# A written-out order for the last four attention units and the last two routing chunks

## The chip, the cores and the metric

The kernel runs on one core of one Trainium2 chip. The metric is the device time of one execution in microseconds (us); the time before is 531.47 us, the median of three runs (531.43 to 533.45).

## The reference

Three steps follow one another, all in fp32. First attention with 4 batches, 8 heads, 768 positions and head width 64: each query sees the 96 keys up to itself and the first 8 keys, with a linear bias in the distance. Its output, 3072 tokens of width 512, goes through a soft mixture of 8 experts with 4 slots each. Its result goes through a feed-forward network with hidden width 2048 and a squared ReLU.

```python
logits = x @ phi                              # 3072 x 32
d = np.exp(logits - logits.max(0)); d /= d.sum(0) + 1e-09
slot_input = d.T @ x                          # 32 x 512
for e in range(E):                            # 8 experts, 4 slots each
    h = np.maximum(slot_input[e] @ w1[e], 0.0)
    slot_out[e] = h @ w2[e]
c = np.exp(logits - logits.max(1)); c /= c.sum(1) + 1e-09
x = c @ slot_out
g = np.maximum(x @ w_in, 0.0) ** 2
out = g @ w_out
```

The softmax `d` runs over all 3072 tokens, so no slot input is final before the last token's attention is done.

## The kernel before

The schedule is manual: each engine works through its instructions in the order in which the program writes them, and waits are put in between for data and for the reuse of tiles.

Attention is cut into 48 units: a batch, a pair of 128-row query tiles, and a pair of heads. Four units (all heads) make a chunk of 256 tokens, so there are 12 chunks; chunk 10 holds units 40 to 43, chunk 11 units 44 to 47. A unit goes through these stages: `stage_qk` (TensorE: scores, line 223), `stage_max` (VectorE: mask and minimum, L236), `stage_exp` (ScalarE: exponentials and their sums, L251), `stage_T` (TensorE: transposes of the probabilities sm, L262), `stage_ev` (VectorE and ScalarE: copies of them out of PSUM, L268), `stage_pv` (TensorE: products with the values, L279), and `stage_x` (ScalarE: copy into the chunk's xT, L289). The loop at L544 takes two units at a time and runs the scores some four units ahead.

`route(k)` (L312) takes a finished chunk to the slots. It is a generator: `queue` and `step(n)` (L489 to 497) place its parts between those of the units. Its steps:

- the logits: products of xT and phi (pt or lt, L351, for an ordinary chunk, copied by L354 and L355 and transposed into pl, L361; directly into pl, L325, for the last chunk);
- the reciprocals rc of the softmax sums (L365, L366), the scaling of the logits by them (L384, or L337) and the head sum into c_tok (L340);
- the turn of xT back to token rows (px, L330) and its scaling into xb (L333);
- pq (L402 or L405), the transposed logits; their running maximum (L420, L421), the exponentials dT and the factor fo for what was summed before (L424, L425);
- pd (L437 or L439), dT transposed back, copied into db (L447); the denominators rden (L456);
- pS (L464), the slot products of db and xb, added to acc with the factor fo (L484).

Odd chunks only do the first three and keep their xb, in the pool `att`; even chunks do the rest for two chunks at once. For chunk 10 (`LAST`) the maximum of its slots is also brought to one row and back (pn, row, pm: L434, L459, L467). Chunk 11 is the tail: `route(11, True)` computes its logits in two halves behind all value products, and then, in the block "last" (L629), pq, dT, pd, the slot products in two matmuls of 512 columns, the sum of acc and pS (L476), and pv (L478), which turns the slot inputs and divides by the denominators. One copy (L479) places them in slotZ, from which the expert products (L654) read. `warm` (L76) issues idle bf16 matmuls; the tail has three, four and six of them (L410, L444, L471).

PSUM has eight banks here: four with tag "s" (scores, and the tail's extra tiles, `bank(..., True)`) and four with tag "m" (all else). Tiles of one tag take its banks in turn, and a new tile waits for the last reader of the one that it replaces.

In SBUF, the pool `att` holds sm (three of 4 KB a partition), raw (queries and keys, four of 3 KB), the value tiles va and vb (two each of 2 KB), pTa and pTb (4 KB each) and the odd chunk's xb; its tags are placed in the order in which they are first asked for: sm, raw, va, pTa, ... Once it is released (L619), the pool `stream` takes its room: s0, s1, s2, each 16 KB a partition, for the second to fourth w2 weights, and slotZ. With `reuse_waits="tile"` each of these waits for the tiles that it lies over. The weight loads (`load_w`, L193; 2 MB each) stand one behind the other on the sync queue (SP): three after the attention, then one behind each expert's products, the last one (w2 of expert 7) in four parts.

## Time and profile before

| what | value |
|---|---|
| median of three runs | 531.47 us |
| the profiled execution | 532.31 us |
| its span, first to last instruction | 530.5 us |
| its mean granted TensorE clock | 0.999 |
| TensorE matmuls busy | 515.5 us, 97% |
| VectorE busy | 383.4 us, 72% |
| ScalarE busy | 306.3 us, 58% |
| GpSimd busy | 167.8 us, 32% |

All times in the views are us from the start of the span, unless marked ns. PE is TensorE, PEld its weight loads, DVE VectorE, ACT ScalarE, POOL GpSimd, SP the sync engine's DMA queue. A row of the timeline merges like instructions that follow one another (x16), with the time from the first's start to the last's end. In brackets stands the idle time of the engine ahead of it and what ended it. An fp32 product shows as two records, a transpose as one. The attention runs to about 177 us, the rest of the routing to 188.9, the experts to about 223, and the feed-forward network from 229 to the end.

### The profile page before, as it was taken

The page shows a single profiled execution, that of the slowest core. Times are in us where ns is not written, and L with a number is a line of the kernel's source. Part 1 is how long each engine was busy: PE and PEld are TensorE (multiplying, and loading weights), DVE is VectorE, ACT ScalarE, POOL GpSimd, SP SyncE. Part 2 cuts the span into 40 slices and gives each one's busy share as a digit, 9 for nine tenths or more (in the row PEclk, how much of TensorE's full clock was granted, in tenths as well). Part 3 has the DMA queues.
Part 4 walks back from the last instruction along what each step waited for, and adds up shares of the span by engine and source line. Part 5 has one row for each costly group of instructions (what it writes and reads, how often), then busy time and mean ns, then how long its engine had stood idle before and what let it go on. Part 6 is the DMA issues. An engine that isn't in the chain of part 4 may idle for free.

```text
span 530.5 us, 10062 instructions
## 1 busy us (share of the span) xinstructions
PE 515.5 (97%) x3628; PEld 392.4 (74%) x3628; DVE 383.4 (72%) x936; ACT 306.3 (58%) x814; POOL 167.8 (32%) x146
## 2 busy tenths in 40 slices
PE   8999999999998899999999999999999999999997
PEld 5787777677776634377787888878888878888885
DVE  5788888787877844778969897967947667545553
ACT  4987877878787201376665655545635445444440
POOL 7000000000000010034674576446554537534441
PEclk9999999999999999999999999999999999999999
DMA  8879999999991799904123021030110000003333
GB/s 281 265 265 314 355 326 342 312 362 314 334 337 43 280 388 416 396 32 160 38 122 121 38 75 84 1 120 0 48 72 1 0 1 1 1 1 120 119 120 119
DMA packets 25977, 89.18 MB, mean 168 GB/s; under 512 B 2882, under 2 KB 3522, under 8 KB 23874
## 3 DMA queue, kind: packets, MB, share of 16 engines
q1 hardware_dynamic: 25776, 88.35, 45.8%
q8 instruction: 30, 0.49, 0.4%
q14 instruction: 25, 0.20, 0.1%
q10 hardware_dynamic: 146, 0.13, 0.1%
HBM read 82.18 MB, written 6.29 MB: 167 GB/s over the span
## 4 chain that ended last, share of the span: by engine, by line
PE 50%; DVE 9%; ACT 1%; issue 1%; POOL 1%; DVEq 0%; POOLq 0%
PE acc L866 14%; PE acc L867 14%; PE acc L868 14%; PE h L848 3%; DVE cvyi L758 1%; DVE rg L853 1%; PE pSO L747 1%; DVE cvyi L757 1%; DVE cvyo L758 1%; DVE oacc L872 1%; PE pre L654 1%; DVE cvyo L757 1%; PE pu L807 1%; DVE winf L761 1%; DVE oacc L874 1%
## 5 line engine op out<-in xcount | busy, mean ns | idle before, releaser
L856 POOL TENSOR_TENSOR g<-rg,g 128x512 fp32r<-128x512 f32 (+1 forms) x109 | 135.1, 1242 | 164.6 <-DVE rg L853 159.6
L866 PE MATMUL acc<-w,g 128*128 128x512 f32 x384 | 151.7, 395 | 1.0 <-DVE oacc L872 1.0
L868 PE MATMUL acc<-w,g 128*128 128x512 f32 x384 | 150.1, 391 | 0.7 <-POOL g L856 0.7
L867 PE MATMUL acc<-w,g 128*128 128x512 f32 x384 | 150.7, 392 | 0.0
L852 ACT ACTIVATE rg<-h 128x512 f32<-128x512 f32 (+1 forms) x109 | 59.7, 548 | 122.2 <-PE h L848 116.0
L874 DVE TENSOR_TENSOR oacc<-acc,oacc 128x512 f32<-128x512 f32 x95 | 65.3, 687 | 58.7 <-PE acc L868 58.7
L251 ACT ACTIVATE sm<-sm,nm 128x256 f32<-128x256 f32 (+1 forms) x192 | 92.8, 488 | 0.3 <-DVE nm L236 0.3
L868 PEld LDWEIGHTS acc<-w,g 128*128 128x128 f32 x384 | 72.1, 188 | 18.5 <-POOL g L856 2.8
L866 PEld LDWEIGHTS acc<-w,g 128*128 128x128 f32 x384 | 72.1, 188 | 17.7 <-DVE oacc L872 1.8
L867 PEld LDWEIGHTS acc<-w,g 128*128 128x128 f32 x384 | 72.4, 189 | 11.1
L853 DVE SCALAR_TENSOR_TENSOR rg<-h,rg 128x512 f32<-128x512 f32 (+1 forms) x109 | 67.8, 622 | 17.2 <-ACT rg L852 17.1
L236 DVE CUSTOM_DVE_ANT_0 sm<-s,mask 128x256 f32<-128x256 f32 (+1 forms) x192 | 66.9, 395 | 3.3 <-ACT sm L251 1.7
L855 ACT ACTIVATE g<-rg 128x512 fp32r<-128x512 f32 (+1 forms) x109 | 63.4, 582 | 3.5
L223 PE MATMUL s<-raw 64*128 64x256 f32 (+1 forms) x384 | 52.6, 394 | 0.7 <-DMA raw<-in_qk 0.7
L628 POOL MEMSET slotZ<- 128x1056 f32 x1 | 1.0, 978 | 155.3 <-DVE nm L236 155.3
L262 PE MATMUL pt<-con,sm 128*128 128x128 f32 x352 | 45.2, 276 | 1.6 <-ACT pT L268 1.6
L279 PE MATMUL o<-pT,v 128*64 128x128 f32 x704 | 44.2, 276 | 0.8 <-issue 0.5
L279 PEld LDWEIGHTS o<-pT,v 128*64 128x64 f32 x704 | 37.9, 137 | 7.9 <-DVE nm L236 2.2
L262 PEld LDWEIGHTS pt<-con,sm 128*128 128x128 f32 x352 | 38.5, 141 | 6.8 <-ACT pT L268 2.8
L223 PEld LDWEIGHTS s<-raw 64*128 64x128 f32 x384 | 31.2, 191 | 15.5 <-DMA v<-in_vx 6.7
L848 PEld LDWEIGHTS h<-cu 128*128 128x128 f32 x192 | 35.8, 188 | 7.4
L848 PE MATMUL h<-cu 128*128 128x256 f32 x192 | 39.8, 280 | 0.0
(166 smaller groups left out, 546.0 us busy)
## 6 DMA issues: line engine op xcount, KB each, us to landing
w<-in_w SPq DMA_DIRECT2D x40, 512.0 KB, 6.7
raw<-in_qk SPq DMA_DIRECT2D x48, 384.0 KB, 5.7
v<-in_vx SPq DMA_DIRECT2D x48, 256.0 KB, 4.5
w<-in_w SPq DMA_DIRECT2D x6, 2048.0 KB, 13.0
out_x<-oacc SPq DMA_DIRECT2D x23, 256.0 KB, 2.0
win<-in_w_in SPq DMA_DIRECT2D x2, 2048.0 KB, 8.9
wout<-in_w_out SPq DMA_DIRECT2D x2, 2048.0 KB, 7.8
win<-in_w_in SPq DMA_DIRECT2D x2, 1536.0 KB, 7.3
```

The costliest lines, as they stand in the source:

```text
L223: nc.tensor.matmul(sc[hh][:, tt, 0:n, :], lhsT=r[r0 : r0 + D, tt, :], rhs=rhs, start=True, stop=True)
L236: V.tensor_tensor_reduce(out=sm[:, j, 0:n, :], in0=sc[hh][:, tt, 0:n, :], in1=m[:, 2:3, :] if n == 1 else m[:, 0:2, :], scale=-QK_SCALE, s ...
L251: nc.scalar.activation(sm[:, j, 0:n, :], sm[:, j, 0:n, :], AF.Exp, bias=nm[:, j : j + 1], scale=-1.0, accum_out=chunk_sums(i // NPR)[:, tt ...
L262: nc.tensor.transpose(pp[tt][:, hh, c, :], sm[:, 2 * tt + hh, c, :], ident)
L279: nc.tensor.matmul(o[hh * D : hh * D + D, tt, :], lhsT=v[:, tt + 2 * c, hh * D : hh * D + D], rhs=pT[:, 2 * tt + hh, c, :], start=c == 0, ...
L848: nc.tensor.matmul(ph[:, k, :], lhsT=U[:, c0 : c0 + P], rhs=cst[:, n * TB : n * TB + TB], start=True, stop=True)
L853: V.scalar_tensor_tensor(g, ph[:, k0:k1, :], 0.0, r, op0=ALU.max, op1=ALU.mult)
L856: G.tensor_tensor(g2[:, 1, js, :], g, g2[:, 0, js, :].bitcast(F32), op=ALU.subtract)
L866: nc.tensor.matmul(pa, lhsT=ghi[:, j, ms], rhs=whi[:, j, :], start=j == 0, stop=False)
L867: nc.tensor.matmul(pa, lhsT=ghi[:, j, ms], rhs=wlo[:, j, :], start=False, stop=False)
L868: nc.tensor.matmul(pa, lhsT=glo[:, j, ms], rhs=whi[:, j, :], start=False, stop=j == J - 1)
L874: V.tensor_tensor(o, pa, o, op=ALU.add)
```

## The change

The loop ends two units earlier, at unit 43, and what was left of the loop and of the generators for chunks 10 and 11 is written out in one order. In it:

- the exponentials of unit 46 come ahead of everything else; the logits of chunk 10 follow the transposes of unit 45, and their copies come ahead of the exponentials of unit 47;
- the transposes of units 46 and 47 are apart, with pl between them;
- the head sum of chunk 10 is three halving adds on GpSimd in place of one reduction on VectorE;
- the logits of chunk 11 are made in two halves, the first (pairs of heads 0 and 1) ahead of the value products of units 46 and 47;
- copies of db are on ScalarE instead of VectorE; row is a row of 32 rather than four copies, and pm has four matmuls in place of one;
- the factor fo of chunk 11 comes ahead of its exponentials;
- the slot products of chunk 11 are four of 256 columns, each on 32 columns of the array, into pS of 128 rows; acc isn't added to them, but has its own products with sdO (fo times the reciprocal) in the two tiles pv, to which the products of the copied pS with sden are added; two copies, one on VectorE and one on ScalarE, place the result;
- the block "last" begins at pr, no longer at pq; of the idle matmuls, three are left ahead of it and two in it;
- the first raw tile is asked for ahead of all other tiles of `att`, and the first value tile after it, so the placing begins raw, va, sm, pTa.

In the diff a line of "..." marks what is left out; the edits of the loop body only drop the conditions on `more_units`.

```diff
+    def raw_tile(i):
+        return att.tile([P, 6, P], F32, tag="raw", name=f"raw{i}", bufs=4)
...
-        r = att.tile([P, 6, P], F32, tag="raw", name=f"raw{i}", bufs=4)
+        r = early.pop("raw", None) if i == 0 else raw_tile(i)
...
+    early = {"raw": raw_tile(0), "v": v_tile(0)}
...
-    early = {"v": v_tile(0)}
...
-            if banks[0] is aps:
-                idle = bank("idle2")
-                warm(3, con, idle)
...
-            if banks[0] is aps:
-                warm(4, con, idle)
...
-            if banks[0] is aps:
-                warm(6, con, idle)
...
-    for i in range(2, NU - 2, 2):
-        more_units = i + 4 < NU
+    for i in range(2, NU - 4, 2):
...
-    i = NU - 2
+    step(1)
+    assert not queue
+    K, L = LAST, LAST + 1
+    i = NU - 4
+    halves = range(2)
+    def logits(bank_, xT, prs):
+        for pr in prs:
+            for t in halves:
+                c0 = (t * 2 + pr % 2) * 2 * NS
+                nc.tensor.matmul(bank_[:, c0 : c0 + 2 * NS], lhsT=xT[:, pr, t * P : t * P + P],
+                                 rhs=phib[:, pr, :, :].rearrange("p a s -> p (a s)"), start=True, stop=True)
+    def by_head(out, in_, rc, h0):
+        n = in_.shape[2]
+        V.tensor_tensor(out, in_, rc[:, :, h0 : h0 + n].unsqueeze(3).broadcast_to([P, 2, n, NS]), op=ALU.mult)
+    def head_sum(out, x):
+        V.tensor_reduce(out, x.rearrange("p t h s -> p t s h"), axis=AX.X, op=ALU.add)
+    def shares(k, tag):
+        rc = post.tile([P, 2, H], F32, tag=tag, name=f"rc{k}")
+        V.tensor_scalar(rc, sums.pop(k), EPS, None, op0=ALU.add)
+        V.reciprocal(rc, rc)
+        return rc
+    def turned(bank_, xT, t):
+        for pr in range(NPR):
+            nc.tensor.transpose(bank_[:, pr * P : pr * P + P], xT[:, pr, t * P : t * P + P], ident)
+    def rows_of(xb, bank_, rc, t):
+        V.tensor_tensor(xb[:, t, :].rearrange("p (h d) -> p h d", d=D), bank_.rearrange("p (h d) -> p h d", d=D),
+                        rc[:, t, :].unsqueeze(2).broadcast_to([P, H, D]), op=ALU.mult)
+    def small(name, shape=(P, 1)):
+        return post.tile(list(shape), F32, tag=name, name=name)
+    stage_exp(i + 2, 0)
+    stage_exp(i + 2, 1)
...
+    xK, xb9 = xTs.pop(K), fronts.pop()
+    pt = [bank(f"lt{K}_{hh}") for hh in halves]
+    for pr in range(NPR):
+        for hh in halves:
+            r = slice(hh * D, hh * D + D)
+            nc.tensor.matmul(pt[hh][pr * NS : pr * NS + NS, 0:TB], lhsT=phib[r, pr, hh, :], rhs=xK[r, pr, :], start=True, stop=True)
...
+    stage_max(i + 3, 0)
...
-    step(1)
+    lt = post.tile([P, 2, TB], F32, tag="lh", name=f"lt{K}")
+    nc.scalar.copy(lt[:, 0, :], pt[0][:, 0:TB])
+    V.tensor_copy(lt[:, 1, :], pt[1][:, 0:TB])
+    stage_max(i + 3, 1)
+    stage_exp(i + 3, 0)
...
+    stage_pv(i + 1)
...
-    stage_pv(i + 1)
-    last = route(NU // NPR - 1, True)
-    next(last)
-    step(1)
+    stage_exp(i + 3, 1)
...
-    step(2)
-    next(last)
-    step(1)
-    next(last)
-    next(last)
-    step(2)
-    queue.append(last)
+    rcK = shares(K, "rc")
+    stage_T(i + 2)
+    stage_ev(i + 2, 0, V.tensor_copy)
+    stage_ev(i + 2, 1, nc.scalar.copy)
+    pl = bank(f"pl{K}")
+    for t in halves:
+        for hh in halves:
+            nc.tensor.transpose(pl[:, (2 * t + hh) * P : (2 * t + hh + 1) * P], lt[:, hh, t * P : t * P + P], ident)
+    stage_T(i + 3)
+    lh = post.tile([P, 2, H, NS], F32, tag="lh", name=f"lh{K}")
+    ph = pl.rearrange("p (t g h s) -> p t h g s", g=2, h=NPR, s=NS)
+    for t in halves:
+        V.tensor_tensor(lh[:, t].rearrange("p (h g) s -> p h g s", g=2), ph[:, t],
+                        rcK[:, t].rearrange("p (h g) -> p h g", g=2).unsqueeze(3).broadcast_to([P, NPR, 2, NS]), op=ALU.mult)
+    stage_ev(i + 3, 0, V.tensor_copy)
+    stage_ev(i + 3, 1, nc.scalar.copy)
+    G.tensor_tensor(lh[:, :, 0:4], lh[:, :, 0:4], lh[:, :, 4:8], op=ALU.add)
+    G.tensor_tensor(lh[:, :, 0:2], lh[:, :, 0:2], lh[:, :, 2:4], op=ALU.add)
+    G.tensor_tensor(c_tok[:, 2 * K : 2 * K + 2, :], lh[:, :, 0, :], lh[:, :, 1, :], op=ALU.add)
+    xL = chunk_x(L)
+    plA = bank(f"plA{L}", True)
+    logits(plA, xL, (0, 1))
+    rcL = shares(L, "rcL")
+    la = att.tile([P, 2, 4, NS], F32, tag="la", name="la", bufs=1)
+    l5 = small("l5", [P, 2, 5, NS])
+    by_head(la, plA.rearrange("p (t h s) -> p t h s", t=4, s=NS)[:, 0:2], rcL, 0)
+    head_sum(l5[:, :, 0, :], la)
+    xbK = post.tile([P, 2, DM], F32, tag="xb", name=f"xb{K}")
+    px = bank(f"px{K}_0")
+    turned(px, xK, 0)
+    rows_of(xbK, px, rcK, 0)
+    stage_pv(i + 2)
+    stage_x(i + 2)
+    px = bank(f"px{K}_1")
+    turned(px, xK, 1)
+    rows_of(xbK, px, rcK, 1)
+    stage_pv(i + 3)
+    stage_x(i + 3)
+    old = run["nm"]
+    pq = bank(f"pq{K}")
+    nc.tensor.transpose(pq[:, 0:P], c_tok[:, 2 * K - 2 : 2 * K + 2, :].rearrange("p t s -> p (t s)"), ident)
+    plB = bank(f"plB{L}", True)
+    logits(plB, xL, (2, 3))
+    mx = small("rmax")
+    nmK = small("nmK")
+    V.tensor_reduce(mx, pq[:, 0:P], axis=AX.X, op=ALU.max)
+    V.scalar_tensor_tensor(nmK, mx, -1.0, old, op0=ALU.mult, op1=ALU.min)
+    dT = post.tile([P, TB], F32, tag="dT", name=f"dT{K}")
+    dnK, foK = small("dn"), small("fo")
+    nc.scalar.activation(dT[:, 0:P], pq[:, 0:P], AF.Exp, bias=nmK, scale=1.0, accum_out=dnK)
+    nc.scalar.activation(foK, old, AF.Exp, bias=nmK, scale=-1.0)
+    by_head(l5[:, :, 1:5, :], plB.rearrange("p (t h s) -> p t h s", t=4, s=NS)[:, 0:2], rcL, 4)
+    head_sum(c_tok[:, 2 * L : 2 * L + 2, :], l5)
+    pn = bank("pn")
+    nc.tensor.transpose(pn[0:1, 0:P], nmK, ident)
+    pd = bank(f"pd{K}")
+    nc.tensor.transpose(pd[:, 0:P], dT[:, 0:P], ident)
+    db = post.tile([P, 4, NS], F32, tag="db", name=f"db{K}")
+    nc.scalar.copy(db, pd[:, 0:P].rearrange("p (t s) -> p t s", s=NS))
+    xbL = post.tile([P, 2, DM], F32, tag="xT", name=f"xb{L}", bufs=2)
+    px = bank(f"px{L}_0", True)
+    turned(px, xL, 0)
+    row = small("row", [1, NS])
+    V.tensor_reduce(row, pn[0:1, 0:P].rearrange("p (g s) -> p s g", s=NS), axis=AX.X, op=ALU.min)
+    rows_of(xbL, px, rcL, 0)
+    px = bank(f"px{L}_1", True)
+    pq = bank(f"pq{L}", True)
+    for t in halves:
+        for g in range(4):
+            nc.tensor.matmul(pq[g * NS : g * NS + NS, t * P : t * P + P], lhsT=c_tok[:, 2 * L + t, :], rhs=ident, start=True, stop=True)
+    pm = bank("pm")
+    for g in range(4):
+        nc.tensor.matmul(pm[g * NS : g * NS + NS, 0:1], lhsT=row, rhs=si[0:1, 0:1], start=True, stop=True)
+    turned(px, xL, 1)
+    pS = bank(f"pS{K}")
+    for t in range(4):
+        nc.tensor.matmul(pS[t * NS : t * NS + NS, :], lhsT=db[:, t, :], rhs=(xb9 if t < 2 else xbK)[:, t % 2, :], start=True, stop=True)
+    idle = bank("idle2")
+    warm(3, con, idle)
+    mxL, nmL = small("rmaxL"), small("nmL")
+    V.tensor_reduce(mxL, pq[:, 0:TB], axis=AX.X, op=ALU.max)
+    V.scalar_tensor_tensor(nmL, mxL, -1.0, pm[:, 0:1], op0=ALU.mult, op1=ALU.min)
+    rows_of(xbL, px, rcL, 1)
+    xTs.pop(L)
+    dnL, foL = small("dnL"), small("foL")
+    nc.scalar.activation(foL, nmK, AF.Exp, bias=nmL, scale=-1.0)
+    dT = post.tile([P, TB], F32, tag="dT", name=f"dT{L}")
+    nc.scalar.activation(dT, pq[:, 0:TB], AF.Exp, bias=nmL, scale=1.0, accum_out=dnL)
+    V.scalar_tensor_tensor(rden, rden, foK, dnK, op0=ALU.mult, op1=ALU.add)
+    V.tensor_tensor(rden, rden, foL, op=ALU.mult)
+    V.scalar_tensor_tensor(acc, acc, foK, pS, op0=ALU.mult, op1=ALU.add)
...
-        step(1000)
+        pr = bank("pr")
+        nc.tensor.matmul(pr[:, 0:1], lhsT=si4, rhs=rden, start=True, stop=True)
+        pd = bank(f"pd{L}")
+        for t in halves:
+            nc.tensor.transpose(pd[:, t * NS : t * NS + NS], dT[0:NS, t * P : t * P + P], ident[0:NS, 0:NS])
+        warm(2, con, idle)
+        db = post.tile([P, 4, NS], F32, tag="db", name=f"db{L}")
+        nc.scalar.copy(db[:, 0:2, :], pd[:, 0 : 2 * NS].rearrange("p (t s) -> p t s", s=NS))
+        rd = small("om")
+        V.tensor_scalar(rd, pr[:, 0:1], dnL, EPS, op0=ALU.add, op1=ALU.add)
+        V.reciprocal(rd, rd)
+        sdO = small("sdO", [P, NS])
+        V.tensor_scalar(sdO, si, rd, foL, op0=ALU.mult, op1=ALU.mult)
+        V.tensor_scalar(sden, si, rd, None, op0=ALU.mult)
+        pS = bank(f"pS{L}", True)
+        for t in halves:
+            for h in halves:
+                r0 = (2 * h + t) * NS
+                nc.tensor.matmul(pS[r0 : r0 + NS, 0:TB], lhsT=db[:, t, :], rhs=xbL[:, t, h * TB : h * TB + TB], start=True, stop=True)
+        pv = [bank(f"pv{h}", True) for h in halves]
+        for kc in range(4):
+            nc.tensor.matmul(pv[kc // 2][:, kc * NS : kc * NS + NS], lhsT=acc[:, kc * P : kc * P + P], rhs=sdO, start=kc % 2 == 0, stop=False)
+        ps = post.tile([P, TB], F32, tag="lh", name="ps")
+        V.tensor_copy(ps, pS[:, 0:TB])
+        z = slotZ.rearrange("p (e r) -> p e r", r=ZS)[:, :, 0 : 4 * NS].rearrange("p e (k s) -> p e k s", s=NS)
+        for c in halves:
+            for h in halves:
+                kc = 2 * h + c
+                R = slice(2 * h * NS, 2 * h * NS + 2 * NS)
+                nc.tensor.matmul(pv[h][:, kc * NS : kc * NS + NS], lhsT=ps[R, c * P : c * P + P], rhs=sden[R], start=False, stop=c == 1)
+        for h, eng in ((0, V.tensor_copy), (1, nc.scalar.copy)):
+            eng(z[:, :, 2 * h : 2 * h + 2, 0:4], pv[h][:, 2 * h * NS : 2 * h * NS + 2 * NS].rearrange("p (k e s) -> p e k s", e=E, s=4))
```

## Rows read from the trace of the kernel before

**Rows 1.** The page, part 1: busy time, share of the span, instructions.
```profile
PE 515.5 (97%) x3628; PEld 392.4 (74%) x3628; DVE 383.4 (72%) x936; ACT 306.3 (58%) x814; POOL 167.8 (32%) x146
```

**Rows 2.** Windows: start:end, us, busy us (instructions) by engine, clock, DMA share, GB/s.
```profile
180.00:185.00 5.00, 3.44 (x40) 2.02 (x32) 4.52 (x12) 0.75 (x3) 0.00 (x0) 1.00 1.01 426
```

**Rows 3.** Timeline, TensorE, 165 to 190 us: start, us, engine, line, operation [idle before].
```profile
165.80 1.97 PE L262 MATMUL pt<-con,sm 128*128 128x128 f32 x16
...
167.69 0.66 PE L351 MATMUL lt<-xT,phib 64*32 64x256 f32 x16
...
171.71 0.66 PE L361 MATMUL pl<-con,lt 128*128 128x128 f32 x4 [1.25 <-ACT lt L354]
...
173.07 1.91 PE L262 MATMUL pt<-con,sm 128*128 128x128 f32 x16
...
175.60 1.97 PE L279 MATMUL o<-pT,v 128*64 128x128 f32 x32 [0.51 <-issue]
...
177.50 1.10 PE L325 MATMUL pl<-phib,xT 128*128 128x64 f32 x8
...
179.60 1.06 PE L464 MATMUL pS<-xb,db 128*32 128x512 f32 x8
...
180.59 0.38 PE L467 MATMUL pm<-con,row 1*128 1x1 f32 x2
...
182.44 0.64 PE L405 MATMUL pq<-con,c_tok 128*32 128x128 f32 x16 [0.89 <-DVE c_tok L340]
...
183.40 0.32 PEld L79 LDWEIGHTS <-con 128*128 128x128 bf16 x3
...
185.72 1.05 PE L464 MATMUL pS<-xb,db 128*32 128x512 f32 x4
...
187.37 1.06 PE L478 MATMUL pv<-sden,acc 128*128 128x32 f32 x8
...
188.88 10.51 PE L654 MATMUL pre<-w,slotZ 128*32 128x512 f32 x96 [0.45 <-DVE slotZ L479]
```

**Rows 4.** ScalarE: the page's exponentials; timeline, a copy, an eviction, and transposes behind it.
```profile
L251 ACT ACTIVATE sm<-sm,nm 128x256 f32<-128x256 f32 (+1 forms) x192 | 92.8, 488 | 0.3 <-DVE nm L236 0.3
...
160.60 0.66 PE L262 MATMUL pt<-con,sm 128*128 128x128 f32 x4 [0.29 <-ACT pT L268]
...
165.24 0.36 ACT L289 COPY xT<-o 128x256 f32<-128x256 f32 x1
...
166.98 0.59 ACT L268 COPY pT<-pt 128x512 f32<-128x512 f32 x1 [1.39 <-PE pt L262]
```

**Rows 5.** Timeline, VectorE and ScalarE: scaling, head sum and exponentials of the last chunk.
```profile
181.25 0.41 DVE L337 TENSOR_TENSOR l<-pl,rc 128x256 f32<-128x256 f32 x1
181.70 0.69 DVE L340 TENSOR_REDUCE c_tok<-l 128x64 f32<-128x320 f32 x1
...
183.89 0.47 ACT L424 ACTIVATE dT<-pq,nm 128x256 f32<-128x256 f32 x1 [5.86 <-DVE nm L421]
```

**Rows 6.** GpSimd by line and shape; timeline of VectorE beside its memset.
```profile
L856 POOL TENSOR_TENSOR g<-rg,g 128x256 fp32r<-128x256 f32 x26 | 21.4, 822 | 39.1 <-DVE rg L853 39.0
...
L149 POOL TENSOR_TENSOR mtmp<-before 128x96 f32<-128x96 f32 x1 | 0.4, 432 | 0.0
...
169.35 0.98 POOL L628 MEMSET slotZ<- 128x1056 f32 x1 [155.33 <-DVE nm L236]
169.46 0.90 DVE L365 TENSOR_SCALAR rc<-sums 128x16 f32<-128x16 f32 x1
```

**Rows 7.** Waits of the sync queue; its issues; TensorE's wait for a weight.
```profile
SPq L204 <- PE pt L262: 9.8, 1, 9.8
...
175.15 0.33 SPq L204 DMA_DIRECT2D w<-in_w  x1
...
180.73 0.33 SPq L204 DMA_DIRECT2D w<-in_w  x1
...
221.53 0.14 PEld L747 LDWEIGHTS pSO<-w,hZ 128*32 128x32 f32 x4 [0.23 <-DMA w<-in_w]
```

More of the change, by code (lines that the diff above doesn't have):

```diff
@@ L553, in attention_moe_ffn @@
         stage_max(i + 3, 0)
-        if more_units:
-            stage_exp(i + 2, 0)
+        stage_exp(i + 2, 0)
         stage_ev(i, 1, nc.scalar.copy)
         stage_ev(i + 1, 0, V.tensor_copy)
-        if more_units:
-            stage_exp(i + 2, 1)
+        stage_exp(i + 2, 1)
         stage_ev(i + 1, 1, nc.scalar.copy)
         stage_max(i + 3, 1)
-        if not more_units:
-            stage_exp(i + 2, 0)
-            stage_exp(i + 2, 1)
-        if more_units:
-            stage_qk(i + 4)
+        stage_qk(i + 4)
         stage_exp(i + 3, 0)
@@ L575, in attention_moe_ffn @@
         step(1)
-        if more_units:
-            stage_max(i + 4, 0)
-            stage_qk(i + 5)
-            stage_max(i + 4, 1)
+        stage_max(i + 4, 0)
+        stage_qk(i + 5)
+        stage_max(i + 4, 1)
         stage_x(i + 1)
@@ L594, in attention_moe_ffn @@
         step(2)
-    i = NU - 2
+    step(1)
[27 more added lines that the diff above has]
+        return post.tile(list(shape), F32, tag=name, name=name)
+    stage_exp(i + 2, 0)
+    stage_exp(i + 2, 1)
     stage_T(i)
     stage_T(i + 1)
+    xK, xb9 = xTs.pop(K), fronts.pop()
[4 more added lines that the diff above has]
+            nc.tensor.matmul(pt[hh][pr * NS : pr * NS + NS, 0:TB], lhsT=phib[r, pr, hh, :], rhs=xK[r, pr, :], start=True, stop=True)
     stage_ev(i, 0, V.tensor_copy)
+    stage_max(i + 3, 0)
     stage_ev(i, 1, nc.scalar.copy)
```

## The prediction

> **What bounds the kernel now.** I read the busy shares first: TensorE is busy 97% of the span [rows 1], so time is lost only where it stands still. The windows then show where: in 180 to 185 us it works 3.44 of 5 us at a granted clock of 1.00 (the upper level, 2.4 GHz), while the DMA share is 1.01 [rows 2]. The timeline of the tail gives the frame: the transposes of units 44 and 45 begin at 165.80, the first expert product at 188.88 [rows 3], so the stretch that the change rewrites takes 23.08 us. Its waits to be seen are 1.25 us for ScalarE's copy ahead of pl at 171.71, and 0.89 us for c_tok of the last chunk at 182.44 [rows 3]. What follows 188.88 isn't edited. It moves with its start, unless a transfer holds it: the only wait for one that the expert stage shows is 0.23 us at 221.53 [rows 7].
>
> So the question is when the first expert product starts. I follow TensorE's queue in the new order with the durations of the old one. Steps are start to start [rows 3]: transposes of two units 1.89 us (165.80 to 167.69), value products of two units 1.90 (175.60 to 177.50), four transposes (pl, or a turn) 0.45 (a third of 171.71 to 173.07), half a chunk's logits 1.05 (half of 177.50 to 179.60); else the duration of the row.
>
> **Part 1: units 44 to 47 and the logits, up to c_tok of chunk 11.** Four exponentials of unit 46 now stand ahead of the evictions of units 44 and 45 on ScalarE. It can start them about 0.26 us after 165.24, at 165.50; four take 1.96 (488 ns each) and the eviction 0.59 [rows 4], so the second half of unit 44 is out at 168.1. The first logits of chunk 10 need its bank: four "m" banks go round, and at 160.60 transposes waited 0.29 us for an eviction in the same way [rows 4]. They start at 168.15 rather than 167.69, a wait of 0.46 us that the change adds; value products are queued behind it. From there the queue runs dense: logits 0.66 to 168.8, value products of 44 and 45 to 170.7, transposes of 46 to 171.65, pl to 172.1, transposes of 47 to 173.05, first half of chunk 11's logits (which needs only units 44 and 45) to 174.1, turn to 174.55, value products of 46 to 175.5, turn to 175.95, value products of 47 to 176.9, pq of chunk 10 to 177.0, second logits to 178.05. The wait for pl is gone, as the copy is now ahead of unit 47's exponentials. What is late next: VectorE needs 0.35 (0.41 less its overlap) and 0.69 for scaling and head sum [rows 5], so c_tok is there at 179.2 with 0.1 for hand-overs; meanwhile TensorE does pn, pd and a turn, until 178.9. pq of chunk 11 starts at 179.25, against 182.44 [rows 3]: **3.2 us earlier.**
>
> **Part 2: the head sum of chunk 10 on GpSimd.** It leaves VectorE; three adds of 256, 128 and 64 elements take its place. Nearest rows: 822 ns for 128x256 and 432 ns for 128x96 [rows 6]. I take 0.8 + 0.5 + 0.35 = 1.65 us (bounds: three of 0.43, three of 0.82); from pl's scaling at 172.95 that is 174.6, and pq of chunk 10 wants it at 176.9. Cover 2.3 us, cost nothing; without it, all 1.65 less the 1.05 that VectorE saves. But VectorE is exposed: a 128x16 scaling took 0.90 us while GpSimd's memset ran from 169.35 to 170.33, and ended with it [rows 6]. In the forecast VectorE gets in after one add, 0.2 us late, hidden, as nothing needs it before 177.2. The Trainium skill (SBUF — State Buffer, section "SBUF: two separate sides") says that VectorE and GpSimd share a port pair under a lock, held for a whole instruction while the other is blocked. The row agrees. By that rule a result of its own is possible, if GpSimd keeps taking the lock; it is the first rival.
>
> **Part 3: from pq of chunk 11 to the end.** TensorE: pq 0.6 to 179.85, eight small pm records 0.35 (two took 0.38, sixteen of pq 0.64 [rows 3]: bounds 0.3 and 0.6), turn 0.45 to 180.65, pS of chunk 10 1.06 to 181.7, three idle matmuls 0.35 to 182.05. Maximum, bias and exponentials of chunk 11 run beside this: before, dT was done 1.28 us after pq's end (183.08 to 184.36 [rows 3, 5]); with 0.3 for fo, now ahead of it, it is ready at 181.4. pr and pd 0.5 to 182.55, the copy of db on ScalarE and hand-overs 0.45 to 183.0. The slot products are now four of 256 columns on four column tiles; four of 512 on four tiles take 1.06, and two of 512 on two tiles 1.05 [rows 3], so tiles run side by side and half the columns give 0.53 (bounds 0.5 and 1.05): 183.55. Then the products of acc, eight records of 128 rows, 1.06 less 0.1 for the last one's end [rows 3], to 184.5; they don't wait for acc plus pS any more, and the copy of pS runs beside them. The four with 64 rows: at most the 1.06 of those, half of it if the two row halves overlap; I take 0.75: 185.25. Copies of the halves on two engines and hand-over 0.45 (before: from 188.43, the products' end, to 188.88): **185.7**, so 6.45 us after pq, where it was 6.44. The boundary of the "last" block now stands between the idle matmuls and pr. Its cost no row shows; before, the longest that it can have hidden is the 0.89 us at 182.44, and nothing excludes zero, as the product started 0.05 us after VectorE's sum [rows 3, 5]. I take 0.2, nearer to that. First expert product at 185.9, **3.0 us earlier.**
>
> **Part 4: what is left out or moved at no cost.** Thirteen idle matmuls go and five come; before, with TensorE at 3.44 of 5 us, the clock stayed at 1.00 [rows 2], and the new queue has fewer holes. GpSimd's memset of slotZ moves behind the adds, to about 175.6; it is needed at 185. VectorE's reciprocals, rows and updates of rden fall into holes of the chain above.
>
> **Part 5: the weight loads.** The sync queue held its first w2 load 9.8 us for a transpose (of unit 47, reading sm), to 175.15, and the third to 180.73 [rows 7]. With raw first, the first region of the stream pool (16 KB a partition) lies over raw (four of 3 KB) and one pair of v (4 KB), read last by the value products of unit 45 at 170.7. So the first load starts some 4.4 us earlier, and the second after unit 46 at 175.5. The third waits for xb of chunk 9, which pS of chunk 10 reads until 181.7: 1 us later than before. Behind it on the queue stand only the loads that wait for the experts. The last load landed 0.23 us late for TensorE at 221.53 [rows 7]; with all 3.0 us earlier it is needed at 218.3. It is issued behind expert 6, so it moves too, and the queue ahead of it is shorter by the 4.4 us of the first load less the 1 us of the third. That lets the gain through; the 0.23 us itself I count at nothing, as no row shows that the stage's end hangs on it.
>
> **Sum.** 3.2 us at pq, nothing from there to the end, less 0.2 for the boundary: 3.0 us. The profiled execution took 532.31 us (span 530.5), 0.84 above the median of 531.47; I take the 3.0 off the median: **528.5 us.** Open bounds: +0.46 if the bank isn't waited for, +0.25 for the 64-row products; -0.7 boundary, -0.5 slot products, -0.3 64-row products, -0.25 pm. Together that is a gain of 1.25 to 3.7.
>
> **Rivals.**
> - *VectorE stands behind GpSimd until adds and memset are through*, at 175.6. Then reciprocal, scaling, sum, both rows of chunk 10 (0.25, 0.35, 0.6, 0.6, 0.65), and its maximum at 178.05 rather than 177.2; c_tok of chunk 11 about 0.8 late. Gain 2.2: 529.3 us. For: the 0.90 us row. Against: between dependent adds GpSimd leaves gaps. Chance 0.12.
> - *The tail keeps a wait of its own*: the boundary costs its 0.89, or db, with pd behind pS, idle matmuls and pr in one queue, comes later than worked out. Gain 0.5 to 1.7, say 530.4 us. For: dT, ready at 181.4, is served only at 182.3. Against: the same queue runs without holes in the forecast. Chance 0.18.
> - *Slower: the w2 loads start later.* If the first region isn't freed by unit 45 but overlaps xb of chunk 9, the in-order sync queue holds all three to 181.7, 6.6 us later than before. The DMA share is 1.01 already [rows 2], so the last load lands about 5 us later (some 1.5 us of holes can be made good), and the wait of 0.23 becomes that: 536 us. It decides as soon as the first load is issued after 175.15. Against: 12 and 4 KB fill the 16 KB exactly. Chance 0.05.
> - *The change doesn't do what it says*, the new order being as long as the old one: 531.5 us, chance 0.03.
>
> **How the numbers follow.** The forecast has 0.62, with its own range of 527.8 to 530.0. A measurement here tells about 0.5% from no change, 2.66 us; the forecast's 3.0 is close above, and it stays above in some five sixths of its cases: 0.52 faster. The rest of it and rivals one, two and four make 0.43 the same; 0.05 slower. The range reaches down to the gain of 3.7 with a little more for the median's own scatter, and up through the second rival: 527.3 to 530.8 us.
>
> **What would show it.** Right: pl without a wait for ScalarE; pq of chunk 11 13.45 us after the transposes of unit 44 (before 16.64); first expert product 20.1 us after them (before 23.08); the first w2 load issued near 170.7 and no wait for w at the last expert; granted clock 1.00 throughout. Wrong: a gap of over 0.5 us at the first logits of chunk 10 or after the idle matmuls; a small scaling on VectorE stretched beside GpSimd; slot products of about 1 us; the expert stage waiting for w.

## The result, and the profile after

In one comparison on one chip the changed kernel took **528.12 us** (median of 5 runs, 527.32 to 528.52) and the kernel before 533.45 (5 runs, 531.43 to 533.61): **ratio 0.991, 95% interval 0.9887 to 0.9934**. The forecast was 528.5 us in a range of 527.3 to 530.8, so the number held. The change was forecast as 3.0 us, and that comparison alone would say 4.8 (0.9% of 533.45). The comparisons told of below, taken together, give a firmer size: 66 runs of the kernel before have a median of 532.0 us and a fastest of 530.48, 20 runs of the changed kernel a median of 528.1 and a fastest of 527.04. That is 3.4 us between the fastest and 3.9 between the medians; the three comparisons that hold both kernels say 3.9 to 4.8. The mean granted clock of a run tells where part of the difference comes from: 38 of 61 runs of the kernel before and 15 of 20 of the changed kernel have 0.998 or more, with medians of 531.1 and 527.7, again 3.4 us apart; in the profiles a mean below 0.998 goes with a stretch at a lower clock, which the last section tells of.

The profiled execution took 527.32 us, with a span of 525.5, against 532.31 and 530.5 before: 5.0 us less. The busy times answer to [rows 1]:

```profile
PE 513.6 (98%) x3638; PEld 392.5 (75%) x3638; DVE 381.1 (73%) x931; ACT 306.8 (58%) x817; POOL 169.3 (32%) x149
```

TensorE's work is 1.9 us less of the 5.0, so most of the gain is idle time. The place is found by cutting the span at two instructions that both kernels have: the transposes of unit 44, called **T44** from here on, and the first expert product. In TensorE's timeline of the changed kernel (start, us, engine, line, operation, in brackets the idle time before it) the stretch reads as follows; it answers to [rows 3].

```profile
164.28 1.97 PE L265 MATMUL pt<-con,sm 128*128 128x128 f32 x16
166.17 1.06 PE L631 MATMUL lt<-xT,phib 64*32 64x256 f32 x16
167.16 1.97 PE L282 MATMUL o<-pT,v 128*64 128x128 f32 x32
169.06 1.09 PE L265 MATMUL pt<-con,sm 128*128 128x128 f32 x8
169.99 0.60 PE L655 MATMUL pl<-con,lt 128*128 128x128 f32 x4
170.43 1.04 PE L265 MATMUL pt<-con,sm 128*128 128x128 f32 x8
171.30 1.00 PE L595 MATMUL plA<-phib,xT 128*128 128x64 f32 x8
...
175.31 0.33 PE L690 MATMUL pq<-con,c_tok 128*128 128x128 f32 x1
...
177.77 0.64 PE L720 MATMUL pq<-con,c_tok 128*32 128x128 f32 x16 [0.29 <-DVE c_tok L603]
178.34 0.24 PE L723 MATMUL pm<-con,row 1*32 1x1 f32 x8
...
180.10 0.50 PE L79 MATMUL idle<-con 128*128 128x256 bf16 x3
180.44 0.29 PE L756 MATMUL pr<-rden,con 128*128 128x1 f32 x2
...
181.32 0.64 PE L773 MATMUL pS<-xb,db 128*32 128x256 f32 x8
181.89 1.08 PE L776 MATMUL pv<-sdO,acc 128*128 128x32 f32 x8
182.90 0.63 PE L784 MATMUL pv<-sden,ps 64*128 64x32 f32 x8
184.00 1.50 PE L809 MATMUL pre<-w,slotZ 128*32 128x512 f32 x12 [0.47 <-ACT slotZ L786]
```

Two brackets are left where [rows 3] has 1.25, 0.51, 0.89 and 0.45: c_tok of chunk 11 (0.29) and the last copy (0.47). T44 to the first expert product is 184.00 - 164.28 = **19.72 us**; it was 188.88 - 165.80 = 23.08. The same stretch as one window (start:end, us, busy us of PE, PEld, DVE, ACT and POOL, clock, DMA share, GB/s), first of the kernel before:

```profile
165.80:188.88 23.08, 19.18 (x209) 14.84 (x207) 16.85 (x47) 9.10 (x31) 0.98 (x1) 1.00 0.61 239
```

and of the changed kernel:

```profile
164.28:184.00 19.72, 18.84 (x218) 14.53 (x217) 14.51 (x42) 9.59 (x34) 2.43 (x4) 1.00 0.75 272
```

TensorE stood still for 23.08 - 19.18 = 3.90 us and now for 0.88: **3.02 of the 3.36 us are idle time**, the other 0.34 less work. Cut once more at pq of chunk 11, the stretch is, before:

```profile
165.80:182.44 16.64, 13.86 (x159) 11.43 (x157) 12.07 (x32) 8.35 (x28) 0.98 (x1) 1.00 0.45 166
182.44:188.88 6.44, 5.32 (x50) 3.41 (x50) 4.78 (x16) 0.75 (x3) 0.00 (x0) 1.00 1.01 429
```

and in the changed kernel:

```profile
164.28:177.77 13.49, 13.11 (x149) 10.93 (x148) 9.99 (x28) 8.42 (x29) 2.43 (x4) 1.00 0.65 235
177.77:184.00 6.23, 5.73 (x69) 3.60 (x70) 4.52 (x15) 1.18 (x5) 0.00 (x0) 1.00 0.96 352
```

Ahead of pq 2.78 us of idle time have become 0.38. Behind it 1.12 have become 0.50, although pS and pm of chunk 10, which stood ahead of pq, now stand there: they took the room of holes and of idle matmuls, which are down from 1.92 us to 0.90. The 0.34 us of less work are therefore 1.02 us fewer idle matmuls and 0.68 us more of all else, the stretched logits of chunk 10 (1.06 for 0.66) included. The rest of the 5.0 us is not the change's: 1.52 us lie ahead of T44 (165.80 against 164.28), where both kernels do the same, and 0.1 behind the first expert product.

Every profiled execution can be split so. Times in us; "to end" is the span less T44; the clock is the lowest five-microsecond window from 180 to 525 us.

| kernel | T44 | pq of chunk 11, after T44 | first expert, after T44 | T44 to end | lowest clock |
|---|---|---|---|---|---|
| before | 165.80 | 16.64 | 23.08 | 364.7 | 1.00 |
| e1_place_only | 164.98 | 16.65 | 23.08 | 364.6 | 1.00 |
| after | 164.28 | 13.49 | 19.72 | 361.2 | 1.00 |
| e3_after_again | 165.86 | 13.49 | 19.73 | 361.6 | 1.00 |
| e12_after_control | 167.35 | 13.49 | 19.73 | 362.9 | 0.66 |
| e2_after_sm_first | 165.14 | 13.49 | 19.72 | 362.7 | 0.66 |
| e4_sum_on_vector | 164.99 | 13.50 | 19.72 | 362.9 | 0.66 |
| e5_exps_behind | 165.03 | 13.91 | 20.15 | 361.7 | 1.00 |
| e6_logits_late | 164.12 | 13.66 | 19.88 | 363.1 | 0.72 |
| e7_old_end | 165.18 | 13.48 | 20.19 | 362.9 | 0.67 |
| e8_no_idle | 165.59 | 13.49 | 20.06 | 365.8 | 0.50 |
| e9_scalar_old_order | 166.85 | 13.91 | 20.14 | 363.2 | 0.75 |
| e10_clock_mid | 166.29 | 13.49 | 19.72 | 361.3 | 1.00 |
| e11_clock_both | 164.83 | 13.50 | 19.73 | 361.4 | 1.00 |

After, e3 and e12 are one and the same kernel. Its tail repeats to 0.01 us; T44 moves by 3.1 us and the part behind by 1.7. An edit in the tail is therefore read from T44, and the total only over many runs.

### The profile page after: what moved, and what is told of

It is laid out like the page before. It is cut to its first block, busy times and chain, and to the rows that moved or that the text cites. A ratio compares the mean times of both kernels' runs of the same rounds, so it can differ in the third digit from the quotient of the medians.

```text
span 525.5 us, 10090 instructions
## 1 busy us (share of the span) xinstructions
PE 513.6 (98%) x3638; PEld 392.5 (75%) x3638; DVE 381.1 (73%) x931; ACT 306.8 (58%) x817; POOL 169.3 (32%) x149
## 4 chain that ended last, share of the span: by engine, by line
PE 51%; DVE 9%; ACT 1%; issue 1%; POOL 1%; DVEq 0%; POOLq 0%
PE acc L1021 15%; PE acc L1022 14%; PE acc L1023 14%; PE h L1003 3%; DVE cvyi L913 1%; DVE rg L1008 1%; PE pSO L902 1%; DVE cvyi L912 1%; DVE cvyo L913 1%; DVE oacc L1027 1%; PE pre L809 1%; DVE cvyo L912 1%; PE pu L962 1%; DVE winf L916 1%; DVE oacc L1029 1%
```

## The experiments

Theories on record before them: the reordered queue gives the gain (mine); the w2 loads, started earlier by the new placing, give it or set its pace; the placing quickens the start of the kernel, which the earlier T44 of the profile pointed to; a single edit carries most of it. The first four runs part the placing and GpSimd from the queue, the next four undo one edit each, the last four ask about ScalarE's order and the clock. Medians with their range and number of runs; the kernel before was at 531.98 (20 runs) beside e1 to e4, 531.27 (30) beside e5 to e8, 533.29 (11) beside e9 to e12.

**e1: the kernel before with raw and v placed first.**

```diff
+    early = {"raw": raw_tile(0), "v": v_tile(0)}
     cmask = att.tile([P, C_W - C_R2], F32, tag="sm", name="cmask", bufs=3)
...
     load_qk(0)
-    early = {"v": v_tile(0)}
     early["pT"] = pT_tile(0)
```

> The kernel before with nothing but the new placing (raw, then va, then sm). Theory A (the order of the tail makes the gain; the 1.5 us that the two profiles differ by ahead of unit 44 are scatter of the start): same time as before, within 0.5 us; the first w2 load is issued some 4.5 us earlier, 4.9 us after the transposes of unit 44 in place of 9.35, and the wait for w at the last expert is gone, but 23.1 us from the transposes of unit 44 to the first expert product stay. Theory B (the placing itself quickens the start): about 1.5 us faster, with the transposes of unit 44 near 164.3 in place of 165.8.

Measured: 532.36 us (530.61 to 534.57, 12 runs), ratio 1.0011 (0.9991 to 1.0032). The sync queue's issue rows of e1:

```profile
169.69 10.56 SPq L207 DMA_DIRECT2D w<-in_w  x3
```

The first w2 load leaves 4.7 us after T44, where the kernel before took 175.15 - 165.80 = 9.35 [rows 3, 7]; no weight is waited for at the last expert; and the time is that of before, 23.08 in the tail and 364.6 behind T44. **Earlier loads alone are worth nothing**, and the start is no quicker over 12 runs.

**e2: the changed kernel in the old placing.**

```diff
-    early = {"raw": raw_tile(0), "v": v_tile(0)}
     cmask = att.tile([P, C_W - C_R2], F32, tag="sm", name="cmask", bufs=3)
     nc.sync.dma_start(cmask, consts[:, C_R2:C_W])
+    early = {"raw": raw_tile(0)}
     load_qk(0)
+    early["v"] = v_tile(0)
```

> The changed kernel with the old placing (sm, then raw). Theory A, with loads that still just set the pace (w is waited for by 0.3 us in the changed kernel too): the tail keeps its 19.7 us, but the first w2 load waits for the transposes of unit 47, some 2.4 us later than in the changed kernel, and the last expert waits for w by 2 us or more: 1.5 to 2 us slower than the changed kernel. Rival C (the loads have room to spare, as the prediction had it): same time as the changed kernel within 0.5 us, no wait over 0.3 us. Theory B: 1.5 us slower by the start alone, with transposes of unit 44 near 165.8.

Measured: 529.22 us (527.16 to 529.65, 6 runs), ratio 0.9929 (0.9907 to 0.995). In its sync queue:

```profile
172.49 9.00 SPq L208 DMA_DIRECT2D w<-in_w  x3
```

The first load is 7.35 us after T44 instead of 4.9, the tail is the same 19.72, and no weight is waited for. My theory expected the later loads to set the pace, with a wait of 2 us or more for w at the last expert; that fell. The loads have room, and the placing is not needed for the gain in the tail. The median is 1.5 us above that of e3 all the same. Four of the six runs have a mean clock of 0.997, the profiled one with its dip near 222 us (last section); the other two, at 1.00, took 527.16 and 527.63, like the runs of e3 at 1.00 (527.04 to 527.80). Whether later loads make that dip more frequent, six runs don't show.

**e3: the changed kernel again**, beside e1, e2 and e4.

> The changed kernel, once more, for the comparison on the same chip. Theory A: 3 to 3.5 us faster than before in the median, 19.7 us from the transposes of unit 44 to the first expert product; those transposes begin anywhere from 164.2 to 165.9. Theory B: they begin at 164.3, and the whole is 4.8 to 5 us faster.

Measured: 527.69 us (527.04 to 531.32, 9 runs), ratio 0.9926 (0.9903 to 0.9949). T44 is at 165.86, as in the kernel before. The 1.5 us that the first pair of profiles showed ahead of T44 was scatter.

**e4: the head sum of chunk 10 back on VectorE.**

```diff
-    G.tensor_tensor(lh[:, :, 0:4], lh[:, :, 0:4], lh[:, :, 4:8], op=ALU.add)
-    G.tensor_tensor(lh[:, :, 0:2], lh[:, :, 0:2], lh[:, :, 2:4], op=ALU.add)
-    G.tensor_tensor(c_tok[:, 2 * K : 2 * K + 2, :], lh[:, :, 0, :], lh[:, :, 1, :], op=ALU.add)
+    head_sum(c_tok[:, 2 * K : 2 * K + 2, :], lh)
```

> The changed kernel with the head sum of chunk 10 as one reduction on VectorE in place of three adds on GpSimd. The prediction's step (hidden in either place): VectorE is busy 1.05 us longer between the eviction of unit 47 and the first half of chunk 11, and nothing needs that before pq of chunk 10: 19.7 us from the transposes of unit 44 to the first expert product, within 0.2, and the small scaling beside it at 0.17 us in place of 0.42. Rival (the sum was on the path): 0.5 to 1 us longer.

Measured: 528.23 us (527.79 to 529.74, 6 runs), ratio 0.9921 (0.9903 to 0.9938); tail 19.72. With the adds on GpSimd, VectorE's and GpSimd's timeline of the changed kernel is:

```profile
171.62 0.73 POOL L664 TENSOR_TENSOR lh<-lh 128x256 f32<-128x256 f32 x1 [157.44 <-PE pt L265]
171.96 0.42 DVE L607 TENSOR_SCALAR rc<-sums 128x16 f32<-128x16 f32 x1
...
172.42 0.46 POOL L665 TENSOR_TENSOR lh<-lh 128x128 f32<-128x128 f32 x1
172.96 0.32 POOL L666 TENSOR_TENSOR c_tok<-lh 128x64 f32<-128x64 f32 x1
```

and with the sum on VectorE, in e4:

```profile
172.67 1.04 DVE L603 TENSOR_REDUCE c_tok<-lh 128x64 f32<-128x512 f32 x1
173.62 0.17 DVE L607 TENSOR_SCALAR rc<-sums 128x16 f32<-128x16 f32 x1
```

The small scaling takes 0.17 us in e4 and 0.42 beside GpSimd, where it ends at 172.38, within 0.03 us of the first add (172.35). It is held for one add and then let in. The Trainium skill (SBUF — State Buffer, section "SBUF: two separate sides") has, for some VectorE operations, an exclusive lock on a port pair shared with GpSimd, held for one whole instruction; the two rows agree. Either way it is hidden: pq of chunk 10 starts at 175.31, 2.0 us after the last add (172.96 + 0.32). **The move to GpSimd is worth 0.00.**

**e5: the exponentials of unit 46 behind the transposes again.**

```diff
-    stage_exp(i + 2, 0)
-    stage_exp(i + 2, 1)
     stage_T(i)
     stage_T(i + 1)
...
+    stage_exp(i + 2, 0)
+    stage_exp(i + 2, 1)
```

> The changed kernel with the four exponentials of unit 46 behind the evictions of units 44 and 45 instead of ahead of everything. The prediction's step (the change adds a wait at the first logits of chunk 10, as their bank waits for an eviction that is late): the 0.4 us by which they take longer (1.06 in place of 0.66) go, and 19.3 us are left from the transposes of unit 44 to the first expert product. Rival (the lost time is made good by a later wait): the exponentials end as late as 168.5 in the changed kernel's times, transposes of unit 46 wait for them, and 19.7 us stay.

Measured: 529.27 us (528.05 to 530.87, 10 runs), ratio 0.9957 (0.9938 to 0.9976). TensorE's timeline of e5:

```profile
166.93 0.66 PE L629 MATMUL lt<-xT,phib 64*32 64x256 f32 x16
167.73 1.97 PE L282 MATMUL o<-pT,v 128*64 128x128 f32 x32
169.63 1.09 PE L265 MATMUL pt<-con,sm 128*128 128x128 f32 x8
170.56 0.60 PE L655 MATMUL pl<-con,lt 128*128 128x128 f32 x4
170.99 1.65 PE L265 MATMUL pt<-con,sm 128*128 128x128 f32 x8
```

The logits of chunk 10 do lose the stretching of the changed kernel (0.66 instead of 1.06), as the prediction had it, but what stands behind them gains only 0.18 (the value products start 2.70 us after T44 instead of 2.88), and the transposes of unit 47 grow from 1.04 to 1.65, waiting for their exponentials. Net the tail is 0.43 us longer: both expectations missed, mine of 19.3 and the rival's 19.7, which had transposes wait, but those of unit 46 and for less. The wait of 0.4 us that the change adds is the cheaper of the two.

**e6: the first half of chunk 11's logits moved back beside the second.**

```diff
-    plA = bank(f"plA{L}", True)
-    logits(plA, xL, (0, 1))
...
+    plA = bank(f"plA{L}", True)
+    logits(plA, xL, (0, 1))
     plB = bank(f"plB{L}", True)
```

(The scaling and sum of that half move with it.)

> The changed kernel with both halves of chunk 11's logits, their scaling and head sum behind the last value products. Theory A (TensorE's queue is dense ahead of c_tok, so what counts is what must follow the last value products): TensorE gains 1.05 us ahead of them and loses it behind; VectorE's scaling and sum of the first half (0.42 + 0.60) come into the chain: 0.6 to 1.1 us more, 20.3 to 20.8 us. Rival (hidden, as TensorE has turns and pS to do): 19.7 us within 0.2.

Measured: 528.84 us (527.26 to 530.66, 10 runs), ratio 0.9952 (0.9929 to 0.9974). TensorE of e6:

```profile
177.78 0.65 PE L720 MATMUL pq<-con,c_tok 128*32 128x128 f32 x16 [0.75 <-DVE c_tok L603]
```

The wait for c_tok grows from 0.29 to 0.75, the tail by only 0.16. My 0.6 to 1.1 missed; the rival, hidden within 0.2, held: TensorE does the logits later instead of earlier, and only 0.16 us of VectorE's work on them comes into the chain.

**e7: the end in its old form**: slot products of 512 columns, acc plus pS on VectorE, then products of 128 rows and one copy.

```diff
-            for h in halves:
-                r0 = (2 * h + t) * NS
-                nc.tensor.matmul(pS[r0 : r0 + NS, 0:TB], lhsT=db[:, t, :], rhs=xbL[:, t, h * TB : h * TB + TB], start=True, stop=True)
...
+            nc.tensor.matmul(pS[t * NS : t * NS + NS, :], lhsT=db[:, t, :], rhs=xbL[:, t, :], start=True, stop=True)
...
+            V.scalar_tensor_tensor(acc[Q, c], acc[Q, c], foL[Q], pS[Q, c], op0=ALU.mult, op1=ALU.add)
```

> The changed kernel with the old end: two slot products of 512 columns on 64 rows, acc added to them in halves on VectorE, one denominators' tile, one copy into slotZ. By the prediction's terms: slot products 1.06 in place of 0.64, then 0.35 + 0.47 for the first half of acc, 1.06 for pv, 0.45: 184.9 in the changed kernel's times, where it starts the experts at 184.0, so 0.9 us more, 20.6 us. Rival (the rows have shown 0.64 us of gain in the end only because pr and pd came early): within 0.3 us of 19.7.

Measured: 529.49 us (528.72 to 530.58, 10 runs), ratio 0.9962 (0.9944 to 0.9979). TensorE of e7:

```profile
183.84 1.08 PE L777 MATMUL pv<-sden,acc 128*128 128x32 f32 x8 [0.58 <-DVE acc L775]
```

The wait for acc is back, and the tail is 0.47 us longer: between my 0.9 and the rival's 0.3 at most. It is the largest price of a single edit in the tail, by this one profile; the totals are taken up below.

**e8: without the five idle matmuls** that are left (nothing else is taken out).

```diff
-    idle = bank("idle2")
-    warm(3, con, idle)
...
-        warm(2, con, idle)
```

> The changed kernel without its five idle matmuls in the tail. Prediction's step (they cost 0.35 and 0.2 us on the queue and the clock doesn't need them): pr and pd 0.35 us earlier, and the first expert product 0.2 to 0.4 us earlier, 19.4 us, granted clock 1.00 throughout the tail. Rival (they keep the clock up): granted clock 0.50 to 0.9 in a window between pq of chunk 11 and the experts, and 1 to 3 us longer.

Measured: 530.65 us (527.57 to 533.35, 10 runs), ratio 0.9971 (0.994 to 1.0002): five runs at 531.4 to 533.4, five at 527.6 to 529.9. The profiled one took 533.23. Windows of e8:

```profile
180.00:183.00 3.00, 2.37 (x24) 1.05 (x23) 2.68 (x10) 0.96 (x4) 0.00 (x0) 1.00 1.03 388
183.00:185.00 2.00, 2.00 (x24) 1.70 (x16) 0.55 (x2) 0.00 (x0) 0.00 (x0) 0.87 0.79 311
185.00:187.00 2.00, 1.53 (x10) 0.50 (x14) 1.69 (x3) 0.21 (x1) 0.00 (x0) 0.50 1.00 393
...
189.00:191.00 2.00, 2.00 (x16) 0.67 (x12) 1.65 (x4) 0.00 (x0) 0.00 (x0) 0.50 0.74 180
191.00:193.00 2.00, 2.00 (x20) 0.54 (x16) 0.00 (x0) 0.00 (x0) 0.00 (x0) 0.92 0.81 319
```

and of the changed kernel:

```profile
185.00:190.00 5.00, 5.00 (x52) 1.75 (x47) 3.10 (x5) 0.84 (x1) 0.56 (x1) 1.00 0.98 365
```

After 2.37 us of work in 3 the granted clock falls to 0.50, the 1.2 GHz level, for nearly seven microseconds (by the shares in the rows, from 184.5 to 191.3); with the idle matmuls it stays at 1.00. T44 to end is 365.8, 4.2 to 4.6 us more than in e3 and after; some 1.4 of it belong to a second such stretch near 227 us (0.66 in the window of 225 to 230), which the last section tells of. The five idle matmuls take 0.90 us of TensorE, all of it in holes. Without them TensorE waits instead:

```profile
181.75 0.35 PE L754 MATMUL pr<-rden,con 128*128 128x1 f32 x2 [0.27 <-DVE rden L738]
182.69 0.64 PE L770 MATMUL pS<-xb,db 128*32 128x256 f32 x8 [0.36 <-ACT db L759]
```

pr starts 2.67 us after pq of chunk 11 in both kernels, so my 0.35 us missed, and the rival held. It doesn't hold for every run: four of the ten have a mean clock of 0.99, like the profiled one, and took 532.6 to 533.4 us, which gives back all that the whole change gains; the other six, at 0.997 and above, took 527.6 to 531.4. Of the 80 runs of all kernels here that keep the five, none is below 0.995.

**e9: ScalarE's old order as a whole**: e5's edit, and the copy of lt behind those exponentials, which the kernel before had as its 1.25 us wait.

```diff
-    nc.scalar.copy(lt[:, 0, :], pt[0][:, 0:TB])
...
+    nc.scalar.copy(lt[:, 0, :], pt[0][:, 0:TB])
```

> The changed kernel with ScalarE's instructions of units 44 to 47 in the order of before: the four exponentials of unit 46 and two of unit 47 ahead of the copy of the logits of chunk 10, the copies of units 44 and 45 and the last two exponentials behind it. Theory D (most of what the change gains ahead of c_tok is ScalarE's order: pl no longer waits for its copy, and the transposes of units 46 and 47 don't wait for exponentials): pl or the transposes of unit 47 wait by 0.7 to 1.2 us, and 20.4 to 20.9 us lie between the transposes of unit 44 and the first expert product, in place of 19.7. Rival (the gain is in the dense queue behind it, whatever ScalarE does): 19.7 to 20.1 us, as with the exponentials alone behind the evictions (20.15).

Measured: 528.32 us (527.85 to 531.77, 6 runs), ratio 0.9915 (0.9894 to 0.9937); tail 20.14, as e5. TensorE of e9:

```profile
172.76 0.66 PE L655 MATMUL pl<-con,lt 128*128 128x128 f32 x4 [0.22 <-ACT lt L641]
```

The wait at pl comes back as 0.22, not 1.25, though pl starts 5.91 us after T44 again, as in the kernel before (172.76 - 166.85 and 171.71 - 165.80). So ScalarE's order isn't what removed the wait in the main; the transposes of unit 46, which now stand ahead of pl on TensorE, cover the copy. Theory D, with 20.4 to 20.9, fell; its rival named the time.

**e10 and e11: more idle matmuls elsewhere.** e10 adds them around the slot transposes near 222 us; e11 does that and adds four at the start of the kernel.

```diff
-    warm(10, zero, idle)
+    warm(12, zero, idle)
...
+    warm(2, zero, idle)
...
-    warm(7, con, idle)
+    warm(14, con, idle)
...
+    warm(6, con, idle)
```

(The first two edits are e11's alone.)

> The changed kernel with seven more idle matmuls behind the last expert product and six behind pst, where TensorE otherwise waits 0.84 and 0.78 us. Theory E (part of the scatter is a granted clock of 0.50 for some 3.4 us around 222 us, seen in some executions only, at 1.4 us each): the executions 1.4 us above the fastest become rare, the median falls by 0 to 1 us against the changed kernel, and the windows from 215 to 230 us show 1.00. Rival (the drop isn't set by these holes): the same distribution as the changed kernel, or 0.1 to 0.3 us slower by the idle matmuls themselves.

> As the kernel with idle matmuls around pst, and two more idle matmuls ahead of the first product of the start and two behind it, where TensorE otherwise waits. Theory E: the products of the first units reach their short duration (0.93 us for eight of 128 columns) earlier or as early, the transposes of unit 44 begin by 165.2 at the latest, and the median falls by a further 0 to 1 us. Rival: the start scatters as before, 164.1 to 165.9, or is 0.2 us later.

Measured: e10 528.89 us (528.0 to 529.73, 6 runs), ratio 0.9918 (0.9901 to 0.9936); e11 528.09 (527.38 to 528.89, 6 runs), ratio 0.9907 (0.989 to 0.9925); both at a clock of 1.00 throughout, as far as 520 us.

**e12: the changed kernel once more**, their control.

> The changed kernel once more, as the control on the same chip: 19.7 us from the transposes of unit 44 to the first expert product; median 527.5 to 528.6 us.

Measured: 529.14 us (527.67 to 532.03, 6 runs), ratio 0.9921 (0.9901 to 0.994). Its profile has a stretch at a lower clock, where e10 and e11 have none. But after and e3 have none either, so one profile each proves nothing; the runs of e11 spread less than e12's, and the intervals overlap. The mean clocks of the runs point theory E's way: all twelve of e10 and e11 have 0.998 or more, while three of e12's six and five of the changed kernel's twenty have less. **Inconclusive** as to the time; no version here is shown to be faster than the changed kernel.

## Why the prediction was right

**The route held, step by step.** pq of chunk 11 came 13.49 us after T44 (forecast 13.45, before 16.64), and from the value products of units 44 and 45 on no step of TensorE's queue up to it strays by more than 0.44 us (the first turn, 7.86 us after T44 for 8.3). The logits of chunk 10 take 0.40 us longer (1.06 less 0.66, forecast 0.46), of which 0.18 reach the value products behind them, as e5 shows. pl has no wait. c_tok of chunk 11 is 0.29 us late, about as forecast (179.25 less 178.9). GpSimd's adds took 0.73 + 0.46 + 0.32 = 1.51 us (forecast 1.65) under a cover of 2.0 (forecast 2.3). The first w2 load left at 169.17, 4.9 us after T44, as forecast, and the third 1.1 us later than before, counted from T44:

```profile
169.17 5.08 SPq L207 DMA_DIRECT2D w<-in_w  x2
...
180.30 0.33 SPq L207 DMA_DIRECT2D w<-in_w  x1
```

**The sum was 0.36 us short.** From pq of chunk 11 to the first expert product it took 6.23 us, where the prediction had 6.45 and 0.2 for the block boundary. The terms that were mis-sized: the boundary cost nothing (pr follows the idle matmuls without a gap, 180.44 in the timeline above), pm took 0.17 instead of 0.35 (178.34 to 178.51), the 64-row products 0.63 instead of 0.75; the other way, the turn took 0.59 instead of 0.45 and the slot products 0.57 instead of 0.53. The 0.35 us that the sum gives the three idle matmuls stand under a wrong name: without them, in e8, pr waits for rden and starts no earlier. The rival by which this part keeps a wait of its own fell: db (0.42 us from 180.90 to 181.32, under two idle matmuls) and the last copy (0.47) were in the sum with 0.45 each.

**The level was 0.5 us low.** The 3.0 us were taken off 531.47, the median of three runs; 66 runs have 532.0. The two errors are of opposite effect on the forecast time, and so it came within 0.4 us of 528.12; that much of the closeness is luck.

**Which edit carries it** the prediction didn't say, and the undoings show that none does: ScalarE's order 0.42 to 0.43, the split logits 0.16, the end 0.47, the sum on GpSimd 0.00, the placing 0.00. That is some 1.05 of the 3.36 us, and a sum of single undoings isn't a share: where one move hides what another would cost, each looks cheap alone. The rest is in what no run undid by itself. I put it down to TensorE's order, in which transposes, value products, turns and logits now stand between the steps of chunk 10's route; e9 speaks for it (the old 1.25 us wait returns as 0.22), but that is argued and not shown. The copies of db on ScalarE, row and pm, fo ahead of the exponentials, the eight idle matmuls fewer and the moved boundary weren't undone either. How much each carries stays open.

These prices are read from the tail. The totals of e5 to e7 would put them higher: they are 2.0 to 2.6 us faster than the kernel before beside them, and e7's fastest run is 1.7 us above the changed kernel's. But no run of the changed kernel stands in that comparison, and T44 alone scatters by 3 us; e9, with a longer tail, even has a lower median than e12 beside it. Why e7's runs lie so high isn't shown.

**Three steps were wrong.** The wait for pl was said to be gone "as the copy is now ahead of unit 47's exponentials"; with the copy behind them, in e9, 0.22 of the 1.25 us return. The idle matmuls that stay were passed over with "the new queue has fewer holes"; without the five, in e8, four of ten runs lose the clock. And the wait for w at the last expert did not go. TensorE's weight loads in the changed kernel:

```profile
PEld pSO L902 <- DMA w<-in_w: 0.3, 1, 0.3
```

It is 0.3 us here, 0.8 in e3 and absent in e12, three executions of one kernel, so the placing doesn't decide it. At 0.3 it cost nothing to be seen: T44 to end is 361.2, against 361.3 and 361.4 in e10 and e11, which have no such wait. In e3 it may be in the 361.6. The slower rival, loads held to the end of xb's use, is refuted by the 169.17, and e2 shows that even 2.5 us later they hold nothing up. The first rival, VectorE behind all of GpSimd's work, fell by the 0.42 us row. That row is also one of the prediction's own signs of being wrong, a small scaling stretched beside GpSimd: it is 0.25 us longer, which part 2 had foreseen with 0.2 as hidden, so the sign told nothing.

## What to carry to other kernels

Where one engine is busy all but a few microseconds of a stretch, follow its queue start to start in the new order with the durations of the old one: that gave 13.45 for 13.49 us. Undo each edit of a bundle alone before crediting any: two of the five here carried nothing, and the sum of the parts was a third of the whole, so the order as a whole has to be tested too. Compare profiles from an instruction behind the start's scatter, and leave a few idle matmuls in holes of the queue until several runs without them show that the clock holds; here six of ten held it, and four did not.
